# DeltaNet with a hard-swish MLP: block products by eleven from block 3, GpSimd's shared additions in two operations, and another pacing of the inversion

## The chip, the core and the metric

The kernel runs on one core of a Trainium2 chip (trn2). The metric is device time in microseconds of one execution. The profile names the engines PE (TensorE), PEld (its weight loads), DVE (VectorE), ACT (ScalarE), POOL (GpSimd) and SP (SyncE, which issues the transfers).

## The reference

Two stages in float32. The first is a delta-rule attention over 4 x 8 heads, 768 tokens, head width 48; the second multiplies its output, as 3072 rows of 384, by two weight matrices with a gate between them:

```python
k_n = k / (norm(k) + 1e-6)
for t in range(768):                     # state: 48 x 48 for each of 32 heads
    y[t]  = q[t] @ state
    state += beta[t] * outer(k_n[t], v[t] - k_n[t] @ state)
x = y.transpose(0, 2, 1, 3).reshape(3072, 384)
h = x @ w_in                             # 384 x 2048
g = h * clip(h + 3, 0, 6) / 6
out = g @ w_out                          # 2048 x 384
```

## The kernel before

**Chunks.** Time is cut into N = 24 chunks of 32 tokens; a chunk holds 4 x 32 = 128 rows on the partitions. For chunk t, `prep` normalises the keys (`kb`, on GpSimd), transposes keys and queries (`pt`), copies them (`KQ`, ScalarE), multiplies them with each other (`sc`) and writes the masked triangles `L` and `LB` on VectorE. The mask times beta (`mb`, function `mask`) and the scaled keys (`bkb`, function `scaled`) are GpSimd's. `chain` then runs the recurrence: `ks` (state times keys and queries) on TensorE, `R` (three VectorE operations at L892 and L898), `pz` (inverse times R, TensorE), `su` (state update, TensorE), `state` (VectorE, L945), and beside them the output: `y` (L811, L854), `py`, and the transposition `yt` into `xT`, the MLP's input.

**Groups.** The triangular inverse X that `pz` needs is made for four chunks at once: groups are chunk 0, chunks 1 to 4, 5 to 8, 9 to 12 and so on. From group 2 on `inverse` does it on VectorE: a transposition in (L461), then 60 column operations in turn (a product L751, a subtraction L756; 30 to 240 elements wide, the widest in the middle), a memset and a transposition out (L465). `pz` of a group's first chunk can't start before that.

**Blocks.** The MLP takes two chunks as a block (256 rows), twelve blocks. The upward product of a block is either `up` (L983: 16 tiles of 3 products 128 columns by 256 rows) or, from block UF = 5 on, `up_by_eleven` (L1055: for each of 8 pairs of tiles, eleven products of 128 x 128 in place of twelve such areas, with sums of the weights, made once by `weight_sums` on GpSimd, and sums of the input, `token_sums` on VectorE). For each pair j, `begin(j)` does four products, which ScalarE copies out (L1069) and GpSimd adds up to shared parts (L1020, in `plus_minus`); `end(j)` does seven more, and VectorE closes with two additions from PSUM (L1085, L1086). ScalarE and VectorE then gate (L1096, L1099; after `up` it is L991 and L994). The downward product from block 2 on is `down_by_seven` (L1211: seven products of half blocks, with sums of g on VectorE, L1197, and additions to the outputs, L1221, most of them by the engine called `near`, GpSimd except in the last block). Two transfers of the outputs, four issues each, follow them.

**Order.** Every engine executes its instructions in the order in which the program writes them. Up to chunk 4 an explicit list sets it. From chunk LS = 5 on a loop over chunks t and NU = 15 units u writes it: each unit takes a step of the chain or of `prep` (`plan`), one unit of the MLP (14 for a downward product, 16 for an upward one, together two chunks), and a number of column operations of the inverse that a budget sets: 

```python
room = max(1.65 - USED[mode["of"]] - CHAIN.get(u, 0), 0.15) / mode["mean"]
due += room * left / max((GS - i) * NU - u, 1)
due = min(due, 3.0)
take(fill, int(due))
```

So an odd chunk goes with a downward product (of block (t - 3)/2), the even chunk after it with the upward product of the next block: chunk 7 with the downward product of block 2, chunk 8 with the upward product of block 3, chunk 11 and 12 with 4 and 5, 15 and 16 with 6 and 7, 19 and 20 with 8 and 9. A group's inverse is spread over the last three chunks of the group before (the one for chunks 9 to 12 over chunks 7 and 8).

## Time and profile before

| what | value |
|---|---|
| median of 3 runs | 677.34 us (676.79 to 678.49) |
| the profiled execution | 677.9 us, its span 676.2 us |
| PE busy | 638.2 us, 94% |
| DVE busy | 500.0 us, 74% |
| ACT, POOL busy | 272.3 us, 221.1 us |
| granted TensorE clock, mean | 0.987 |

The profiled execution lies 0.56 us above the median; 1.7 us of it are outside the span. PE's busy time counts modelled ends, so it is read together with the waits. Busy shares are averages: the first 130 us (loading, converting weights) differ from the stretch from 213 us on, in which a pair of one downward and one upward product repeats about every 50 us.

### The profile page before, as it was taken

How to read it: one execution, taken by the hardware profiler on the slowest of the kernel's cores; microseconds unless marked ns; L12 is line 12 of the kernel's file. 1: busy time of each engine (PE TensorE's matmuls, PEld its weight loads, DVE VectorE, ACT ScalarE, POOL GpSimd, SP SyncE). 2: the span in 40 equal slices, each digit the busy share in tenths (PEclk: the TensorE clock that was granted, in tenths of full speed). 3: DMA queues.
4: the chain of work that ended last, by engine and by line, in shares of the span. 5: the costliest groups of instructions: out<-in, count | busy, mean ns of one | idle time of the engine just before them, and what ended most of it. 6: DMA issues, size and time to landing. Idle time of an engine off the chain costs nothing.

```text
span 676.2 us, 26940 instructions
## 1 busy us (share of the span) xinstructions
PE 638.2 (94%) x11768; PEld 579.8 (86%) x11768; DVE 500.0 (74%) x1226; ACT 272.3 (40%) x532; POOL 221.1 (33%) x376
## 2 busy tenths in 40 slices
PE   2568989999999999999999999999999999999997
PEld 2457977776689988988999999999999999999997
DVE  5998867888546699747888957998747998557264
ACT  5995767422143132232244244244244143143250
POOL 6230232002521121236165255065052151442340
PEclk9978989999999999999999999999999999999999
DMA  7896435402041030032030030020020020010000
GB/s 190 214 231 147 97 75 147 82 1 48 17 87 22 3 71 3 2 72 37 3 71 4 3 73 2 3 61 2 3 49 3 2 49 2 15 25 3 26 1 23
DMA packets 88501, 33.29 MB, mean 49 GB/s; under 512 B 80160, under 2 KB 83232, under 8 KB 88384
## 3 DMA queue, kind: packets, MB, share of 16 engines
q1 hardware_dynamic: 88128, 31.29, 20.4%
q8 instruction: 92, 1.51, 0.9%
q10 hardware_dynamic: 256, 0.30, 0.2%
q14 instruction: 25, 0.20, 0.1%
HBM read 26.84 MB, written 4.72 MB: 47 GB/s over the span
## 4 chain that ended last, share of the span: by engine, by line
PE 82%; DMA 6%; DVE 6%; issue 2%; ACT 1%; SPq 1%; POOL 1%; DVEq 0%; ACTq 0%; POOLq 0%
PE po L1211 27%; PE ph L1055 17%; PE ph L983 15%; PE po L1146 6%; PE ks L798 3%; DMA w_out<-in_moe_w_in_dram 3%; PE py L819 3%; PE pz L819 3%; PE su L927 3%; PE pt L518 2%; PE sc L539 2%; DMA qb<-in_q_dram 1%; PE yt L864 1%; DVE A L756 1%; DVE pr L751 1%
## 5 line engine op out<-in xcount | busy, mean ns | idle before, releaser
L1055 PE MATMUL ph<-xT,w_in 128*128 128x128 f32 x784 | 122.9, 278 | 0.0
L983 PE MATMUL ph<-xT,w_in 128*128 128x256 f32 (+1 forms) x576 | 117.0, 356 | 0.7 <-ACT spare L348 0.5
L1211 PE MATMUL po<-w_out,g 128*128 128x192 f32 x640 | 110.6, 326 | 0.0
L983 PEld LDWEIGHTS ph<-xT,w_in 128*128 128x128 f32 x576 | 96.3, 197 | 12.6 <-DVE g L994 0.6
L1055 PEld LDWEIGHTS ph<-xT,w_in 128*128 128x128 f32 x784 | 103.9, 192 | 1.3
L1020 POOL TENSOR_TENSOR g<-g 128x128 f32<-128x128 f32 x168 | 79.7, 476 | 75.4 <-ACT g L1069 66.2
L1211 PEld LDWEIGHTS po<-w_out,g 128*128 128x128 f32 x640 | 104.1, 190 | 0.2
L1211 PE MATMUL po<-spare,g 128*128 128x192 f32 x480 | 86.7, 332 | 0.0
L1211 PEld LDWEIGHTS po<-spare,g 128*128 128x128 f32 x480 | 77.2, 190 | 1.8
L1221 POOL TENSOR_TENSOR o<-o,u 128x192 f32<-128x192 f32 x18 | 18.6, 1035 | 167.2 <-ACT o L1218 93.5
L991 ACT ACTIVATE g<-ph,halves 128x256 f32<-128x256 f32 (+1 forms) x96 | 41.2, 437 | 78.3 <-PE ph L983 78.1
L1069 ACT ACTIVATE g<-ph 128x512 f32<-128x512 f32 x56 | 33.4, 597 | 80.5 <-PE ph L1055 77.0
L1197 DVE TENSOR_TENSOR g<-g 128x256 f32<-128x256 f32 x160 | 62.7, 440 | 3.5 <-PE po L1211 3.1
L756 DVE TENSOR_TENSOR A<-A,pr 128x30 f32<-128x30 f32 (+9 forms) x150 | 59.5, 397 | 3.6
L751 DVE TENSOR_TENSOR pr<-A 128x30 f32<-128x30 f32 (+9 forms) x150 | 56.1, 374 | 3.4
L994 DVE SCALAR_TENSOR_TENSOR g<-g,ph 128x256 f32<-128x256 f32 (+1 forms) x96 | 35.0, 371 | 25.2 <-ACT g L991 24.7
L348 ACT ACTIVATE spare<-spare,places 128x768 uint16<-128x768 uint16 (+1 forms) x56 | 52.5, 941 | 1.6 <-DMA spare<-in_moe_w_in_dram 0.6
L1099 DVE SCALAR_TENSOR_TENSOR g<-o,g 128x512 f32<-128x512 f32 x56 | 42.5, 759 | 6.6 <-ACT o L1096 6.6
L1218 ACT ACTIVATE o<-po 128x192 f32<-128x192 f32 x40 | 13.3, 331 | 80.5 <-PE po L1211 76.3
L1146 PE MATMUL po<-w_out,g 128*128 128x384 f32 x128 | 45.6, 493 | 0.0
L1096 ACT ACTIVATE o<-g,halves 128x512 f32<-128x512 f32 x56 | 40.5, 722 | 12.6 <-DVE g L1099 8.9
L478 POOL TENSOR_TENSOR mb<-beta_tok,mask 128x256 f32<-128x256 f32 x38 | 27.0, 730 | 55.8 <-DVE LB L550 55.8
(141 smaller groups left out, 985.2 us busy)
## 6 DMA issues: line engine op xcount, KB each, us to landing
kf<-in_k_dram SPq DMA_DIRECT2D x96, 48.0 KB, 2.8
qb<-in_q_dram SPq DMA_DIRECT2D x96, 48.0 KB, 2.8
vf<-in_v_dram SPq DMA_DIRECT2D x96, 48.0 KB, 2.1
out_dram<-o SPq DMA_DIRECT2D x92, 48.0 KB, 1.6
spare<-in_moe_w_in_dram SPq DMA_DIRECT2D x4, 768.0 KB, 7.7
w_out<-in_moe_w_in_dram SPq DMA_DIRECT2D x4, 768.0 KB, 8.0
w_out<-in_moe_w_out_dram SPq DMA_DIRECT2D x4, 768.0 KB, 5.6
spare<-in_moe_w_out_dram SPq DMA_DIRECT2D x4, 768.0 KB, 4.4
```

Of the source, the lines that this page charges most:

```text
L348: nc.scalar.activation(out=z, in_=z if n else d.bitcast(I16)[:, :, :, 3], func=func, bias=places[:, n : n + 1], scale=scale,)
L751: nc.vector.tensor_tensor(out=pv, in0=A[:, j + 1 :, j].unsqueeze(2).to_broadcast([n, w, j]), in1=A[:, j, 0:j].unsqueeze(1).to_broadcast([n ...
L756: nc.vector.tensor_tensor(out=A[:, j + 1 :, 0:j], in0=A[:, j + 1 :, 0:j], in1=pv, op=ALU.subtract)
L819: nc.tensor.matmul(ps[rows(place(b)), D * h : D * h + D], lhsT=m(h)[rows(b)], rhs=z[rows(b), D * at(h) : D * at(h) + D], start=True, stop= ...
L983: nc.tensor.matmul(ph[:, cols], lhsT=w_in[:, s, f * 128 : (f + 1) * 128], rhs=xT[:, s, cols], start=(s == 0), stop=(s == NKT - 1),)
L991: nc.scalar.activation(out=g, in_=ph, func=ACTF.Relu, bias=half, scale=1.0 / 6.0)
L1020: nc.gpsimd.tensor_tensor(out=out, in0=a, in1=b, op=op)
L1055: nc.tensor.matmul(ph[:, n], lhsT=w, rhs=x, start=start, stop=stop, skip_group_check=True)
L1099: nc.vector.scalar_tensor_tensor(out=g, in0=r, scalar=1.0, in1=g, op0=ALU.min, op1=ALU.mult)
L1146: nc.tensor.matmul(pos[c][:], lhsT=gs[blk, f // 2][:, f % 2, c * P : (c + 1) * P], rhs=w_out[:, f, :], start=(f == 0), stop=(f == NFC - 1),)
L1197: nc.vector.tensor_tensor(out=A(f, *out), in0=A(f, *a), in1=A(f, *b), op=op)
L1211: nc.tensor.matmul(ps[n][:], lhsT=A(f - f % 2, *a)[:, f % 2], rhs=b[:, f], start=(f == 0), stop=(f == HF - 1),)
```

## The change

Five edits. (1) `up_by_eleven` from block 3 on in place of 5, which moves `weight_sums` from the downward product of block 4 to that of block 2 and brings `token_sums` to blocks 3 and 4. (2) The shared parts of a pair in two GpSimd operations (one of 128 x 256, one of 128 x 128) in place of three of 128 x 128, and the closing additions in the other order. (3) All `near` additions on VectorE. (4) The GpSimd masks two units later, after the copy of the transposed keys. (5) Another budget for the columns: other means, more units marked in CHAIN, and half a unit less in units 11 to 13 of odd chunks.

```diff
-        if whole:
-            drain(mask(t))
         yield                                   # prep, after kb
...
+            if whole and j == 0:
+                drain(mask(t))                  # prep, after the copy of KQ
             yield
...
-    mode = {"of": "down", "mean": 0.72}
+    mode = {"of": "down", "mean": 0.6}
...
-    UF = 5
+    UF = 3
...
-            plus_minus(gt[:, 1], gt[:, 1], gt[:, 2], ALU.add)
-            plus_minus(gt[:, 2], gt[:, 0], gt[:, 1], ALU.add)
-            plus_minus(gt[:, 0], gt[:, 0], gt[:, 3], ALU.add)
+            plus_minus(gt[:, 3:1:-1], gt[:, 0:2], gt[:, 3:1:-1], ALU.add)
+            plus_minus(gt[:, 0], gt[:, 0], gt[:, 2], ALU.add)
...
-            nc.vector.tensor_tensor(out=gt[:, 3], in0=ph[:, 3], in1=gt[:, 2], op=ALU.add)
             nc.vector.tensor_tensor(
                 out=gt[:, 1:3], in0=ph[:, 1:3],
-                in1=gt[:, 0].unsqueeze(1).to_broadcast([128, 2, P]), op=ALU.add,
+                in1=gt[:, 3].unsqueeze(1).to_broadcast([128, 2, P]), op=ALU.add,
             )
+            nc.vector.tensor_tensor(out=gt[:, 3], in0=ph[:, 3], in1=gt[:, 0], op=ALU.add)
...
-        near = nc.gpsimd if blk + 1 < N // CB else nc.vector
+        near = nc.vector
...
-            mode["mean"] = 0.72 if blk + 1 < UF else 0.45
+            mode["mean"] = 0.6 if blk + 1 < UF else 0.4
...
-        CHAIN = {1: 0.75, 2: 0.75, 3: 0.4, 4: 0.4, 6: 0.8, 9: 0.8, 10: 0.8}
+        CHAIN = {
+            0: 0.8, 1: 0.8, 2: 0.7, 3: 0.4, 4: 0.4, 5: 0.4, 6: 0.4, 9: 0.8, 10: 0.8, 13: 0.3, 14: 0.4
+        }
...
-                room = max(1.65 - USED[mode["of"]] - CHAIN.get(u, 0), 0.15) / mode["mean"]
+                room = max(1.65 - USED[mode["of"]] - CHAIN.get(u, 0) - (0.5 if t % CB and 10 < u < 14 else 0), 0.15) / mode["mean"]
```

Counted in the programs, between the R of one chunk and the R of the next, the column operations fall so: 

| | chunk 7 | 8 | 9 | 10 | 11 | 12 | 14 | 15 | 16 | 18 | 19 | 20 |
|---|---|---|---|---|---|---|---|---|---|---|---|---|
| before | 27 | 31 | 0 | 16 | 26 | 18 | 15 | 26 | 19 | 15 | 26 | 19 |
| after | 24 | 32 | 4 | 11 | 22 | 27 | 11 | 22 | 27 | 11 | 22 | 27 |

(two of the first group lie in chunk 6 before the change).

## The prediction

> **What bounds the kernel.** I read the page first (busy shares, slices), then busy time by stretches, one from each block's first downward product to the next. DVE 74% as a mean hides that it is nearly full wherever an inverse runs:

> ```profile
> PE 638.2 (94%) x11768; PEld 579.8 (86%) x11768; DVE 500.0 (74%) x1226; ACT 272.3 (40%) x532; POOL 221.1 (33%) x376
> ...
> 213.07:264.88 51.81, 51.58 (x872) 46.11 (x871) 42.10 (x110) 14.39 (x31) 9.75 (x14) 1.00 0.12 25
> 264.88:316.02 51.14, 51.14 (x872) 46.27 (x871) 33.16 (x76) 14.57 (x32) 22.04 (x31) 1.00 0.19 37
> 316.02:367.25 51.23, 50.53 (x952) 48.51 (x951) 44.61 (x112) 17.73 (x37) 21.13 (x37) 1.00 0.12 26
> 367.25:417.48 50.23, 50.19 (x953) 48.38 (x951) 37.20 (x85) 19.27 (x40) 23.15 (x41) 1.00 0.13 26
> 417.48:469.63 52.15, 50.51 (x951) 48.46 (x951) 47.79 (x119) 19.07 (x39) 22.33 (x39) 1.00 0.10 21
> ```

> After the interval the columns are PE, PEld, DVE, ACT, POOL busy, clock, DMA. PE is the bound, with no gap in the second row and few elsewhere; the clock is full. An undisturbed stretch with `up` takes 51.14 us, one with eleven 50.23. DVE has 4 to 7 us left where an inverse runs (rows 3 and 5).

> Next the chain that ended last, for what each product costs TensorE when nothing interrupts it:

> ```profile
> 297.82 2.59 PE ph L983 x12
> ...
> 634.50 19.71 PE ph L1055 x176
> ```

> Then the timelines of DVE and PE over chunks 11 to 13:

> ```profile
> 347.96 0.52 DVE L756 TENSOR_TENSOR A<-A,pr 128x210 f32<-128x210 f32 x1
> 348.40 0.73 DVE L892 SCALAR_TENSOR_TENSOR R<-ks,parity,vf 128x192 f32<-128x192 f32 x2
> 351.71 0.74 DVE L811 SCALAR_TENSOR_TENSOR y<-ks,parity,y 128x192 f32<-128x192 f32 x2 [0.79 <-ACT y L835]
> 365.80 0.29 DVE L1085 TENSOR_TENSOR g<-ph,g 128x128 f32<-128x128 f32 x1 [1.13 <-PE ph L1055]
> 366.46 1.23 DVE L1099 SCALAR_TENSOR_TENSOR g<-o,g 128x512 f32<-128x512 f32 x1
> 373.40 1.99 DVE L465 STREAM_TRANSPOSE X<-A 128x1024 f32<-128x1024 f32 x1
> 376.49 0.62 DVE L898 SCALAR_TENSOR_TENSOR R<-ks,parity,R 128x384 f32<-128x384 f32 x1
> ...
> 453.64 0.88 PE L819 MATMUL pz<-R,X 32*32 32x48 f32 x64 [0.83 <-DVE R L898]
> ```

> Two deadlines tie DVE to PE. `pz` of an even chunk waits for R, which stands behind columns (first line): PE stood 0.15, 0.83 and 0.83 us for it, in chunks 12, 16 and 20. `pz` of a group's first chunk waits for the transposed inverse and R behind it: R ended at 377.1, `pz` started at 377.25, so nothing is in hand there.

> **TensorE's work.** `up` is 96 passes at 2.59/12 = 0.216 us: 20.7 us. Eleven is 176 passes in 19.71. A block gains 1.0 us (the two undisturbed stretches differ by 0.91; I use 0.95), two blocks 1.9. In the last stretch weight loads were busy 19.52 of 19.71 us, so narrower products save less than their columns: by columns alone 176 x 0.108 = 19.0 would save 1.7 a block. [...] The trace's spacing is 112 ns, and the sum uses it.

> **VectorE's work.** An eleven block costs 8 x (0.285 + 0.425 + about 0.74) = 11.6 us and 1.9 of token sums, against 16 x 0.417 = 6.7 for `up`: +7 us in each of blocks 3 and 4. The five `near` additions cost DVE 0.355 each (the last block's), 1.8 a block, and GpSimd loses 4.0 (1.04 + 0.64 and so on). These lie in odd chunks, where DVE waits 1 to 3 us a chunk for products; price if that is gone: 1.8 a block. The outputs' transfers wait for the last but one of them. On SP eight issues (4.3 us) and then the loads of v and q stand behind; R of the even chunk doesn't use those loads (at 396.11 it ran while they were being issued), so a few tenths of delay are covered by a chunk.

> **GpSimd.** A pair goes from three operations (1.52 us) to 0.73 (the 128x256 row of the weight sums) + 0.45: 0.3 less, 2.7 an even chunk. Its effect is through DVE: operations with both inputs in SBUF run slower while GpSimd works (L756 0.53 against 0.35, L1099 1.23 against 0.68), those from PSUM don't. The weight sums (16 x 0.73 = 11.7 us) move to chunk 7, where POOL is busy 9.8 of 51.8; kb, mask and bkb queue behind some, and are early by more than 5 us. Masks later: shared parts stop queueing behind 1.2 us of mask; L waits for `sc` anyway. All at nothing; were the cover gone, 1 to 2 us once for the sums.

> **Columns.** This decides. Ahead of R in chunk 12 twelve columns stood after the last output addition; five will, so R comes right after `ks`, and the 1.81 us of PE waits go. But DVE then idles: R is done at about D + 29.7 (D is the block's first downward product), and the next closing pair needs `end(1)`, at D + 32.1 (399.38 - 367.25 in chunk 14, which has no columns there). `y` starts when ScalarE has its part, at D + 35.7 (351.71 - 316.02) in either kernel. Behind `y` in chunk 12 stand 26 columns instead of 18: 8 x 0.43 = 3.4 us more. Waits in that stretch absorb 0.45 + 1.13 = 1.6. So X, and `pz` of chunk 13, come 1.8 us later than D + 61.2.
> Chunk 17: R of chunk 16 had been late, `y` at D + 36.8 comes 1.1 earlier, waits absorb 0.45 + 0.80: 3.4 - 1.3 - 1.1 = +1.0. Chunk 21: waits 0.19 + 1.15, `y` 0.8 earlier: +1.3.
> Chunk 9, whose group runs through blocks 2 and 3 in two chunks only: behind `y` of chunk 8 stand 29 columns and 4 more after it, 15 more than in chunk 12's pattern, 15 x 0.43 = 6.5. D + 61.2 + 6.5 - 1.6 = D + 66.1, against D + 61.7 before (274.77 - 213.07): +4.4. Block 4's gain of 0.95 follows in the next stretch; block 3's is inside.
> Sum: 4.4 + 1.8 + 1.0 + 1.3 - 0.95 = +7.5.

> Against it: GpSimd slowed DVE in chunk 12 by about 2.5 us (three gatings 0.5 each, columns 1.0). How much of that remains no row shows. Bounds: all (0 gained) or none (2.5 a group, 10 in all). In proportion to GpSimd's time (15.0 to 12.3 us an even chunk) 0.45 would go; with the mask no longer ahead of the shared parts, and the gatings elsewhere in the queue, I take 1.0 a group, 4.0 in all. That gives +3.5: 677.9 + 3.5 = 681.4 for a profiled execution, 0.56 less for the median, **680.8**.

> **Rivals.** (a) *VectorE catches up*: with contention gone as good as wholly (over 2 us a group, the point from which it decides) X is in time in chunks 13, 17 and 21 and TensorE's own work sets the pace: -1.9 for two blocks, -1.81 for R, -0.44 for the wait in chunk 15 at 427.88, all of it lost again only where chunk 9 waits. Full: 677.3 - 4.2 = 673.2; with 1.9 lost in chunk 9: 675. For it: the second row above, with GpSimd busy 22.04 us but mostly outside DVE's busy spells, has no PE gap at all. Against: the anchors at D + 32.1 and D + 35.7 are TensorE's and ScalarE's, whatever DVE has left, and the columns stand behind them.
> (b) *Work saved and columns late cancel*: contention falls by about 1.7 a group, +0.7: 678.
> (c) *Odd chunks lose as well*: 3 more columns and one output addition stand ahead of `y` in chunks 11, 15 and 19 (16 against 13): 1.65 us later, where chunk 15 had no idle time in its queue; `yt` and `begin(0)` then wait, up to 1.3 a group: 680.8 + 4 = 684.8.

> **How the numbers follow.** Forecast 0.45, (a) 0.30, (b) 0.20, (c) 0.05. The range 673.0 to 684.0 takes in (a) and contention unchanged (684.8) but for its end. A measurement of this kernel tells about 0.3% (2 us) from no change: faster 0.30 is (a), same 0.21 is (b) and the edge of the forecast, slower 0.49 is the rest.

> **What would show it.** Right: PE waits of 3 to 5 us at `pz` of chunk 9 (releaser R or the transposition) and 1 to 2 us in chunks 13, 17 and 21; none at `pz` of 12, 16, 20; DVE idle 2 us after R there; DVE over 48 us in the stretches of chunks 7 to 8. Wrong: PE without gaps there, stretches of 50.2 us from block 2 on, or L756 and L1099 at their undisturbed 0.35 and 0.68 throughout.

## The result, and the profile after

The changed kernel took **696.76 us** (median of 4 runs, 695.79 to 698.13) against 677.37 before (4 runs): ratio **1.0286**, 95% interval 1.0263 to 1.0309. Slower was the right side, but the prediction had 680.8 and a range that ended at 684.0. The loss is 19 us, not 3.5.

First the page of the kernel after, its busy shares and one of its DMA queues (packets, MB, share):

```profile
PE 641.1 (92%) x11928; PEld 587.5 (85%) x11928; DVE 516.8 (74%) x1295; ACT 280.7 (40%) x548; POOL 193.7 (28%) x307
...
q8 instruction: 94, 1.54, 0.9%
```

PE is busy only 2.9 us longer than before, in a span that is 17.9 us longer: TensorE mostly waits. The second line becomes important below. Busy time by stretches, cut at the first downward product of each block (columns as in the prediction: PE, PEld, DVE, ACT, POOL, clock, DMA):

```profile
214.07:270.30 56.23, 52.16 (x952) 50.07 (x950) 45.40 (x112) 17.71 (x37) 23.05 (x35) 0.97 0.12 24
270.30:326.27 55.97, 52.69 (x953) 50.76 (x951) 41.98 (x101) 19.28 (x40) 17.51 (x27) 0.94 0.17 34
326.27:379.96 53.69, 50.97 (x952) 48.44 (x951) 46.18 (x119) 18.74 (x39) 15.61 (x25) 1.00 0.12 25
379.96:431.64 51.68, 50.19 (x953) 48.38 (x951) 38.56 (x95) 19.16 (x40) 18.64 (x28) 1.00 0.12 25
```

Before, these four took 51.81, 51.14, 51.23 and 50.23 us. The clock, 1.00 in all four before, is 0.97 and 0.94 in the first two. Where TensorE stands still, the timeline of PE shows (in brackets: idle time ahead, and what ended it):

```profile
252.37 0.34 PE L539 MATMUL sc<-KQ 64*32 64x64 f32 x14 [1.88 <-issue]
264.29 0.52 PE L864 MATMUL yt<-ident,y 128*128 128x128 f32 x3 [2.19 <-DVE y L854]
283.70 1.50 PE L819 MATMUL pz<-R,X 32*32 32x48 f32 x64 [3.28 <-DVE X L465]
364.32 0.33 PE L539 MATMUL sc<-KQ 64*32 64x64 f32 x10 [0.97 <-issue]
375.56 0.55 PE L864 MATMUL yt<-ident,y 128*128 128x128 f32 x3 [1.52 <-DVE y L854]
391.58 0.88 PE L819 MATMUL pz<-R,X 32*32 32x48 f32 x64 [1.49 <-DVE R L898]
```

Three kinds of stop: `pz`, which the prediction named; `yt`, which it did not; and stops inside `sc`, between two of 64 like products, with no releaser ("issue"). The first two come again in chunks 16 and 17 (1.55, 1.49) and 20 and 21 (1.69, 0.80). The third line has one thing more: the same 64 products take 1.50 us there and 0.88 in the last. The clock says why:

```profile
264.00:265.50 1.50, 1.21 (x11) 1.24 (x12) 1.47 (x5) 0.49 (x1) 0.00 (x0) 1.00 0.00 0
265.50:267.00 1.50, 1.50 (x9) 1.50 (x9) 1.47 (x4) 1.20 (x3) 0.56 (x1) 0.52 0.00 0
267.00:268.50 1.50, 1.50 (x9) 1.50 (x8) 0.44 (x1) 0.28 (x1) 1.42 (x3) 0.50 0.00 0
...
286.00:287.50 1.50, 1.50 (x27) 1.33 (x12) 1.20 (x5) 0.00 (x0) 0.00 (x0) 0.50 0.00 0
```

Behind the 2.19 us at `yt` the granted clock is 0.50 until about 269, behind the 3.28 at `pz` until about 289: 1.7 and 2.9 us lost, worked out from busy time and clock of 1.5 us slices.

The balance from 214 to 672 us: stops at `yt` 6.95, at `pz` 7.06, inside `sc` 2.85, one of 0.23 for `KQ`, together 17.1 against 3.4 before; plus 4.6 for the clock; less 1.8 that eleven saves in the two blocks (x1 below). That makes 16.5; the stretches grew by 16.7. (Another 1.2 us lies ahead of 214 us, where traces differ by up to 6.)

### The profile page after: what moved, and what is told of

Its sections match the earlier page's. It is cut to its first block, busy times and chain, and to the rows that moved or that the text cites. A ratio compares the mean times of both kernels' runs of the same rounds, so it can differ in the third digit from the quotient of the medians.

```text
span 694.1 us, 27284 instructions
## 1 busy us (share of the span) xinstructions
PE 641.1 (92%) x11928; PEld 587.5 (85%) x11928; DVE 516.8 (74%) x1295; ACT 280.7 (40%) x548; POOL 193.7 (28%) x307
## 3 DMA queue, kind: packets, MB, share of 16 engines
q8 instruction: 94, 1.54, 0.9%
## 4 chain that ended last, share of the span: by engine, by line
PE 75%; DVE 15%; issue 4%; ACT 3%; DMA 1%; SPq 0%; POOL 0%; DVEq 0%; ACTq 0%; POOLq 0%
PE po L1210 23%; PE ph L1055 21%; PE ph L983 8%; PE po L1145 6%; PE pz L819 3%; PE ks L798 3%; DVE A L756 2%; PE sc L539 2%; PE py L819 2%; PE pt L516 2%; DVE g L1098 2%; DVE pr L751 2%; PE su L927 2%; ACT spare L348 1%; DVE g L1084 1%
## 5 line engine op out<-in xcount | busy, mean ns | idle before, releaser
L1020 POOL TENSOR_TENSOR g<-g 128x256 f32<-128x256 f32 (+1 forms) x144 | 87.4, 608 | 292.4 <-ACT g L1069 286.8
L1055 PE MATMUL ph<-xT,w_in 128*128 128x128 f32 x1008 | 159.8, 280 | 0.4 <-ACT KQ L524 0.2
L1055 PEld LDWEIGHTS ph<-xT,w_in 128*128 128x128 f32 x1008 | 135.0, 193 | 2.4 <-ACT KQ L524 0.8
L1069 ACT ACTIVATE g<-ph 128x512 f32<-128x512 f32 x72 | 43.0, 597 | 109.5 <-PE ph L1055 106.4
L1084 DVE TENSOR_TENSOR g<-ph,g 128x256 f32<-128x256 f32 x72 | 30.2, 420 | 61.7 <-PE ph L1055 40.3
L983 PE MATMUL ph<-xT,w_in 128*128 128x128 f32 (+1 forms) x384 | 71.2, 337 | 2.3 <-DVE g L994 1.6
L983 PEld LDWEIGHTS ph<-xT,w_in 128*128 128x128 f32 x384 | 59.4, 195 | 9.5 <-DVE g L994 2.0
L756 DVE TENSOR_TENSOR A<-A,pr 128x30 f32<-128x30 f32 (+9 forms) x150 | 59.6, 398 | 3.6
L1098 DVE SCALAR_TENSOR_TENSOR g<-o,g 128x512 f32<-128x512 f32 x72 | 53.1, 738 | 7.7 <-ACT o L1095 7.6
L1095 ACT ACTIVATE o<-g,halves 128x512 f32<-128x512 f32 x72 | 52.0, 723 | 11.8 <-DVE g L1098 7.4
L1055 PE MATMUL ph<-beta_tok,sums_in 128*128 128x128 f32 x288 | 55.7, 275 | 0.0
L1055 PEld LDWEIGHTS ph<-beta_tok,sums_in 128*128 128x128 f32 x288 | 43.7, 192 | 0.0
L524 ACT ACTIVATE KQ<-pt 128x512 f32<-128x512 f32 x48 | 27.8, 593 | 36.3 <-PE pt L516 35.7
```

The lines of the kernel that those rows point to most:

```text
L756: nc.vector.tensor_tensor(out=A[:, j + 1 :, 0:j], in0=A[:, j + 1 :, 0:j], in1=pv, op=ALU.subtract)
L983: nc.tensor.matmul(ph[:, cols], lhsT=w_in[:, s, f * 128 : (f + 1) * 128], rhs=xT[:, s, cols], start=(s == 0), stop=(s == NKT - 1),)
L1020: nc.gpsimd.tensor_tensor(out=out, in0=a, in1=b, op=op)
L1055: nc.tensor.matmul(ph[:, n], lhsT=w, rhs=x, start=start, stop=stop, skip_group_check=True)
L1069: nc.scalar.activation(out=gt, in_=ph[:], func=ACTF.Copy)
L1095: nc.scalar.activation(out=r, in_=g, func=ACTF.Relu, bias=half, scale=1.0 / 6.0)
```

## The experiments

The medians of before were 679.9 to 680.5 us on the chips that ran these, so ratios are compared; an expectation in us stands for its ratio to 677.4. Durations of stretches come from one trace for each kernel. Where no stop lies in them they agree from kernel to kernel (51.14, 51.14 and 51.13 for chunks 9 and 10 in the table), but stops inside `sc` differ between kernels with the same products (0.97 to 2.07 us in chunk 12), and the traced execution of e2 lay 4.2 us above its median. The eight from chunk 7 to chunk 22, summed: before 399.6, the changed kernel 416.3.

| stretch (chunks) | before | f1 budget | e1 all but UF | e4 UF alone | after | x1 after, no columns |
|---|---|---|---|---|---|---|
| 7, 8 | 51.81 | 51.63 | 52.14 | 56.58 | 56.23 | 51.93 |
| 9, 10 | 51.14 | 51.14 | 51.13 | 53.25 | 55.97 | 50.11 |
| 11, 12 | 51.23 | 52.15 | 51.84 | 55.21 | 53.69 | 51.64 |
| 13 to 22 | 245.4 | 250.2 | 249.9 | 245.4 | 250.4 | 244.0 |
| sum | 399.6 | 405.2 | 405.0 | 410.4 | 416.3 | 397.7 |

### The change taken apart: e1, e4, f1, e2, e3, g1

**e1_uf5**, the changed kernel with `up` back in blocks 3 and 4:

```diff
-    UF = 3
+    UF = 5
```

> The changed kernel with eleven products from block 5 again (UF = 5), all else as changed. Theory 1 (columns behind y: the budget puts 8 more columns behind y of chunks 12, 16 and 20, and the eleven products of block 3 on top of that overload chunk 8): the two stretches from block 2 on, 9.2 us over before in the changed kernel, come back, the three groups after that stay: 696.8 - 9.2 = 687.5, with waits of TensorE at yt of chunks 12, 16, 20 (1.5 us each) and at pz of chunks 13, 17, 21. Rival A (the near additions on VectorE are what delays y): 690 or more, since blocks 2 and 3 keep them too. Rival B (the eleven products in blocks 3 and 4 alone): back to 677 to 679.

Measured 1.0079 (1.0041 to 1.0117), less than theory 1 had (687.5, ratio 1.015) and more than rival B. The stops are those of theory 1: the first two stretches come back, and `yt` and `pz` of the later groups still wait (1.50, 1.56, 1.70 and 1.15, 1.49, 0.78). **e4_uf3_only**, the kernel before with edit (1) alone:

```diff
-    UF = 5
+    UF = 3
```

> The kernel before with eleven products from block 3 on, all else as before. Theory 1: chunk 8 has 27 columns and the closings behind y, chunk 9 is late by about half of what the changed kernel shows, the groups after that are as before: 677.4 + 3 to 5 = 680 to 682, with a TensorE wait at pz of chunk 9 of 1 to 3 us. Rival B (block 3 alone costs the whole of the 9.2 us): 686. Rival C (TensorE's saved work is worth its 1.9 us because the old budget keeps VectorE in time): 675.5.

Measured 1.0178 (1.0132 to 1.0224), above all three expectations. Two stops inside `sc` (2.04 and 1.97 us in chunks 8 and 12), each with half clock behind it, were in none of them; `pz` of chunk 9 waits 2.12. **f1_pace_only**, the kernel before with edit (5) alone:

```diff
-    ... CHAIN = {1: 0.75, 2: 0.75, 3: 0.4, 4: 0.4, 6: 0.8, 9: 0.8, 10: 0.8}; means 0.72, 0.45
+    ... CHAIN as in the change; means 0.6, 0.4; 0.5 less in units 11 to 13 of odd chunks
```

> The kernel before with the new budget for columns alone (the dictionary, the 0.5 for odd chunks, 0.6 and 0.4). Theory (the budget costs what is left of the loss when blocks three and four keep up): as e1, ratio 1.007, waits at yt of chunks 12, 16 and 20 (1.5 us) and at pz of 13, 17 and 21 (0.8 to 1.5 us). Rival (two-operation shared parts, masks or the near additions cost it): ratio 1.000 to 1.003, no wait over 0.8 us at yt.

Measured 1.0098 (1.0062 to 1.0133), with the stops it was to have (the `yt` of chunks 16 and 20 1.56 and 1.03, `pz` of 17 and 21 1.76 and 0.78):

```profile
366.17 0.55 PE L864 MATMUL yt<-ident,y 128*128 128x128 f32 x3 [1.50 <-DVE y L854]
382.12 0.88 PE L819 MATMUL pz<-R,X 32*32 32x48 f32 x64 [1.43 <-DVE R L898]
```

So the loss has two parts that add up. The budget costs 5.6 us of stretches (f1 less before); eleven from block 3 costs 11.3 (after less e1) or 10.8 (e4 less before); the other three edits together nothing beside the new budget (e1 less f1: -0.1). Beside the old one the traces have 1.5 us (g1 less before) and 3.1 (e2 less e4) for them; the medians of e2 and e4, 1.0140 and 1.0178, don't bear out the second.

**e2_pace_b**, the changed kernel with the budget of before (f1's diff, reversed):

> The changed kernel with the budget of before (means, CHAIN, no subtraction in odd chunks), all else as changed. Columns then: 30 and 27 in chunks 7 and 8, 26 and 19 in chunks 11 and 12. Theory 1 (budget): the waits at yt of 12, 16, 20 and pz of 13, 17, 21 go (3.0 us a group, 7.5 in all with what the later stretches show), and of the 9.2 in blocks 2 and 3 half goes with 5 columns fewer behind y and no clock loss: 684 to 685; R of even chunks waits behind columns again (0.8 each). Rival A (near additions): 693 or more. Rival B (eleven products in blocks 3 and 4): 687, the first two stretches unchanged at 56 us.

Measured 1.0140 (1.0087 to 1.0192). The stops at `yt` of 12, 16 and 20 and `pz` of 13, 17 and 21 go, but for 0.2 us, and those at `pz` of 12, 16 and 20 return (1.10, 1.23, 1.63), with one at `pz` of 8 (1.74). The first two stretches give back half of the 9.2 us, as theory 1 had it (55.49 and 52.04). By time it is rival B all the same (1.0140 is 687): stops inside `sc` of chunks 12 and 16 (2.07, 1.85), each with half clock behind it, come on top. **e3_near_b**, the changed kernel with `near` on GpSimd again:

```diff
-        near = nc.vector
+        near = nc.gpsimd if blk + 1 < N // CB else nc.vector
```

> The changed kernel with the near additions on GpSimd again, all else as changed. Theory 1 (columns behind y): near additions lie in odd chunks, in which VectorE waits for products, so little changes: 694 to 697. Rival A (near additions delay VectorE into the even chunk, 1.8 us a block): 696.8 - 4 x 1.8 = 689 to 690 or lower.

Measured 1.0264 (1.0218 to 1.0310), not to be told from the changed kernel: the additions cost nothing. **g1_two_mask**, edits (2) and (4) on the kernel before (their lines as in the change):

> The kernel before with the shared parts in two GpSimd operations (and the closing additions that go with them) and the masks later; budget, near additions and the number of up blocks stay. Theory: these two cost nothing, 0.998 to 1.001, since GpSimd is not on the path and the budget alone (1.0098) was as dear as everything but the up blocks (1.0079). Rival (they shift work into VectorE's busy spells, as e2 against e4 could be read): 1.003 to 1.005, with longer waits in front of pz of chunks 12, 16 and 20 than 0.8 us.

Measured 1.0029 (1.0007 to 1.0051), just under the rival's range: a little slower, where the theory expected nothing. `pz` of chunks 12 and 20 waits 1.10 and 1.23, as the rival had it; in chunk 16 it is `KQ` that waits, 1.31.

### With VectorE out of the way: x1, x2

**x1_nocol_after** and **x2_nocol_before** skip the columns of the four inverses from chunk 9 on:

```diff
         for j in range(1, C - 1):
             w = C - 1 - j
+            if first(g) >= 9:
+                yield
+                yield
+                continue
```

> The changed kernel without the column operations of the inverse for the groups that begin with chunk 9 and later (their two VectorE operations a column are left out, the schedule's places for them stay). Theory one (VectorE's queue: the columns stand ahead of what TensorE waits for): the waits of TensorE in front of yt and pz from 260 us on go, and with them the half clock behind the two longest: 2.2 + 3.3 + 1.5 + 1.5 + 1.6 + 1.5 + 1.7 + 0.8 = 14.1 us, and about 3 us for the clock, so about 679.5, ratio 1.003; the two stops inside sc (1.9 and 1.0 us, released by nothing in the profile) stay at the same matmuls. Rival (TensorE's own side or the data's arrival is what makes it late): over 690, ratio over 1.018, waits in front of yt and pz still there.

> The kernel before without the same column operations. Only its own waits can go (0.2 + 0.15 + 0.8 + 0.4 + 0.8 = 2.4 us): 675, ratio 0.9965. Beside x1 it gives what eleven products in blocks three and four are worth with VectorE out of the way: the prediction said 1.9 us less; with the stops in sc that the changed kernel shows (2.9 us in all) x1 would come out 1 us above x2, without any other loss.

x1: 0.9984 (0.9955 to 1.0014). x2: 0.9934 (0.9904 to 0.9964). Both are a little under what was expected (1.003 and 0.9965). All waits for VectorE go, and no slice of 5 us between 200 and 670 shows a lower clock. The stretch of chunks 9 and 10, of x1 and then of x2:

```profile
266.54:316.65 50.11, 50.11 (x952) 48.35 (x951) 36.98 (x83) 19.25 (x40) 19.36 (x29) 1.00 0.19 38
```

```profile
266.94:318.07 51.13, 51.13 (x871) 46.27 (x870) 30.44 (x65) 14.57 (x32) 22.02 (x31) 1.00 0.19 37
```

Both full. Eleven saves 1.02 us in block 4, as predicted (0.95), and 0.8 in block 3 (51.93 less its stop of 1.59, against 51.13 in x2). x1 has only the stops inside `sc` left, 1.59, 1.29 and 1.50 us in chunks 8, 12 and 16, more than the two blocks save. The eight stretches are 2.9 us longer in x1 than in x2 (397.7 against 394.8), and 16.7 with the columns. So most of the change's loss needs the columns in VectorE's queue; the stops inside `sc` do not.

### The stops inside sc: p1

How many TensorE records lie ahead of such a stop, read as the first count in the row from 0 to just before it: after (chunk 8), e4 (chunk 8), x1 (chunk 16).

```profile
0.00:252.30 252.30, 218.59 (x4796) 180.03 (x4797) 190.12 (x470) 128.15 (x229) 76.44 (x126) 0.99 0.41 95
```

```profile
0.00:256.10 256.10, 221.99 (x4796) 183.25 (x4797) 196.03 (x473) 128.64 (x229) 81.25 (x135) 0.95 0.41 94
```

```profile
0.00:456.30 456.30, 421.18 (x8604) 374.94 (x8605) 311.39 (x746) 204.65 (x387) 145.79 (x230) 0.99 0.29 65
```

Where eleven starts with block 3, such stops come at 4796 in chunk 8, 6700 in chunk 12 and 8604 in chunk 16, and in the first 100 us of all kernels at some of 349, 475, 727, 853, 979 and 2002 (the changed kernel has all six): mostly steps of 126 to 127 or a multiple, and 11928 records over the 94 packets of queue q8 are 126.9. So the stops are as far apart as one packet of that queue (1.54 MB / 94 = 16 KB) is long, counted in records. **p1_pad18** moves the program against that grid:

```diff
-            for p in range(NP):
+            for p in [0] * (18 if t == j == 0 else 0) + list(range(NP)):
                 nc.tensor.transpose(
```

> The changed kernel with the first of the transpositions into pt in chunk 0 issued 18 times more at the start (the same result written again), so that everything behind it on TensorE stands 18 matmuls later in the instruction stream; the trace shows each as two records, 36 in all. Theory (the stops without a releaser sit at fixed places of the instruction stream: in every kernel so far behind records 349, 475, 727, 853, 979, 2002, 4796, 6700, 8604, many of them multiples of 126 to 127 apart): the stops in sc of chunks 8 and 12 go, others may turn up 36 records earlier in the sequence. If they lie on the path that sets the end, 1 to 3 us less than the changed kernel, ratio to before 1.024 to 1.027; where the wait in front of yt of chunk 8 only grows by what the stop loses, the first 1.9 us bring nothing. Rival (the stop belongs to sc, to its banks or its operands): they stay in sc of chunks 8 and 12.

Measured 1.0303 (1.0264 to 1.0342). The padding made 18 records (11946 in place of 11928), not 36. `sc` of chunks 8 and 12 runs whole, and a stop shows in chunk 13, which had none; behind it the count:

```profile
253.56 0.86 PE L539 MATMUL sc<-KQ 64*32 64x64 f32 x64
...
393.97 0.21 PE L539 MATMUL sc<-KQ 64*32 64x64 f32 x1 [2.10 <-issue]
```

```profile
0.00:393.90 393.90, 352.65 (x7208) 309.11 (x7209) 304.92 (x750) 177.57 (x332) 122.02 (x192) 0.94 0.31 70
```

7208 is 6700 + 4 x 127: the new stop lies on the same grid, so the stops belong to places in the instruction stream and not to one `sc`. The longest of them after 200 us took 2.66 us (k1, below).

Why a place stops TensorE in one kernel and not in another, the times of the packets of q8 in the traces say. From 200 us on the kernels have 33 stops of this kind of 0.25 us or more. Each ended 1.2 to 1.6 us after the transfer of a packet had ended, and 2.3 to 2.9 us after it had begun. In the changed kernel that packet came from 249.81 to 250.92 us, and TensorE, which had reached 4796 at 250.49, went on at 252.37. In d1 (below) the packet was there at 251.04 and TensorE reached the same product at about 252.9; in p1, where 4796 still lies inside `sc` of chunk 8 (records 4764 to 4828), the packet was there at 250.03 and TensorE at about 254.0. Neither stopped. So in these three traces TensorE stood where it came to the place before the packet had landed, and ran on where it came after. `pz` and `sc` use up 128 records in 1.6 us (as do `su` and `py`), less than the 2.3 to 2.9 us from a packet's start to the end of a stop; 128 products of L1055 take an estimated 14 us (at 19.71/176 each). What sets the moment at which a packet is called for the runs do not say.

The padding brought no time: the waits at `yt` and `pz` of chunks 8 and 9 grew to 2.58 and 3.68, and three new stops came.

### What a stop costs beside its length: t1

**t1_stops** is x2 with the first two operations of R repeated in six even chunks:

```diff
+            for e in [0, 1] * {10: 4, 12: 5, 14: 6, 16: 7, 18: 8, 20: 10}.get(t, 0):
+                nc.vector.scalar_tensor_tensor(...)   # as the two of R above
```

> What a stop of TensorE costs beside its length: the kernel of x2 (no columns from the group of chunk 9 on, so no waits of its own), with the first two operations of R issued again 4, 5, 6, 7, 8 and 10 times in chunks 10, 12, 14, 16, 18 and 20, 0.33 us each operation, so that pz comes late by some 1.7, 2.3, 3.0, 3.6, 4.3 and 5.6 us, each stop alone, 50 us from the next. Theory (a stop of about 2 us or more can halve the granted clock for some 3.5 us, and one of over 3 us does): full clock in chunk 10, 0.5 for 3 to 6 us after the last three, the rest open; x2 plus the stops (20.5 us) plus 1.7 to 3 us for each halved clock: 701 to 708. Rival (the drops in the runs so far had another cause, such as two stops close together): clock 1.00 throughout, 695.

Measured 1.0403 (1.0370 to 1.0436), 707.3 us. Chunk 10 had room for its repetitions; the others stopped PE for 2.14, 3.29, 3.55, 5.86 and 6.33 us. Clock behind the first two and in the fourth:

```profile
356.55:358.05 1.50, 1.50 (x128) 1.44 (x128) 1.47 (x5) 0.49 (x1) 0.00 (x0) 1.00 0.51 98
...
410.03:411.53 1.50, 1.50 (x72) 1.38 (x79) 1.47 (x5) 0.00 (x0) 0.00 (x0) 0.50 0.46 87
...
526.13:527.63 1.50, 1.50 (x9) 1.50 (x8) 0.00 (x0) 0.93 (x3) 0.28 (x1) 0.50 0.00 0
```

Against x2 the stretches grew by 2.56, 4.65, 6.49, 8.81 and 8.60 us: the stop of 2.1, with one of 0.24 for `KQ` in the same stretch, costs 0.2 more than the two, one of 3.3 costs 1.4 more, the longer ones 2.3 to 3.0 more.

Length alone does not decide: 2.19 us was enough in the changed kernel at 264, while 2.58 (p1) and 3.29 (e3) passed at full clock. The traces show more. In each of them the granted clock changes only at times that lie a multiple of 3.41 us apart; in the changed kernel that is at 265.56, 268.97, 282.62 and 289.45. Read in these windows, the 2.19 us of the changed kernel fall into one, and the 3.29 us of e3 into two:

```profile
262.14:265.56 3.42, 1.27 (x12) 1.30 (x13) 3.28 (x9) 0.49 (x1) 0.45 (x1) 1.00 0.00 0
265.56:268.97 3.41, 3.41 (x19) 3.41 (x18) 1.99 (x5) 1.49 (x3) 2.45 (x4) 0.50 0.02 5
```

```profile
280.33:283.74 3.41, 1.46 (x9) 1.17 (x8) 3.31 (x11) 0.91 (x2) 1.42 (x2) 1.00 0.00 0
283.74:287.15 3.41, 2.07 (x131) 1.94 (x132) 3.41 (x9) 0.49 (x1) 0.00 (x0) 1.00 0.02 5
```

From 115 to 660 us the 20 traces hold 3037 such windows at full clock. All 16 in which PE stood for 1.96 us or more had half clock in the next, and none with less than 1.62 had. Of the 19 between, 8 had: they held 41 to 130 products, mostly short ones, and 10 of the other 11 held 9 to 16 wide ones. So what told these stops apart was how much of one fell into a single window and, between 1.62 and 1.96 us, which products stood beside it.

### Block four alone, and the weight sums: u4, b1, s1

**u4_uf4_only** is the kernel before with UF = 4; **b1_uf4_two_mask** adds edits (2) and (4).

```diff
-    UF = 5
+    UF = 4
```

(What these expectations call chunks 10 and 11 is the stretch from 264.7 us, chunks 9 and 10 in the table; likewise one chunk less for the one ahead of it.)

> The kernel before with eleven products from block four on (the stretch of chunks 10 and 11, where no inverse is due; block three, in the stretch of chunks 8 and 9 that ends with an inverse, keeps up). Theory (block three is what pushes the inverse; block four alone has room): the stretch of chunks 10 and 11 goes from 51.1 to 50.2 us, ratio 0.997 to 0.9995; a stop at a page of instructions can take 1 to 2 us of it away, since everything behind stands 80 records later. Rival (any eleven block where up stood costs VectorE more than it has): a wait of over 1 us at yt or pz in chunks 10 to 13, ratio over 1.003.

> Both together: eleven from block four on, two-operation shared parts and late masks, on the kernel before. If both theories hold, as u4 within 0.002: 0.996 to 1.000, the candidate for a version that beats both.

u4 1.0063 (1.0043 to 1.0083), b1 1.0108 (1.0081 to 1.0136): both missed. u4 has the rival's ratio without its waits: none over 0.4 us at `yt` or `pz` in chunks 10 to 13, but 1.52 for `KQ` of chunk 12. b1 loses as u4 does, 1.7 us more in front of products of `up`, with half clock behind 1.68 us at `pz` of chunk 20. u4 lost 1.8 us in the stretch of chunks 7 and 8, where it still has `up`. Its timeline there, GpSimd and VectorE:

```profile
260.28 0.75 POOL L1020 TENSOR_TENSOR sums_in<-w_in,sums_in 128x256 f32<-128x256 f32 x1
260.69 0.57 DVE L756 TENSOR_TENSOR A<-A,pr 128x210 f32<-128x210 f32 x1
260.99 0.86 POOL L1020 TENSOR_TENSOR w_in<-w_in 128x256 f32<-128x256 f32 x1
261.30 0.77 DVE L751 TENSOR_TENSOR pr<-A 128x198 f32<-128x198 f32 x1
262.10 0.77 DVE L756 TENSOR_TENSOR A<-A,pr 128x198 f32<-128x198 f32 x1
...
265.17 0.54 DVE L854 TENSOR_TENSOR y<-y,py 128x384 f32<-128x384 f32 x1
```

The weight sums, written down with the next downward product, ran 11 us ahead of it on an idle GpSimd, beside the columns: the product of 198 columns took 0.77 us, and 0.37 in the kernel before. **s1_uf4_sums_late** makes the sums wait for the last `up`, and puts `near` on VectorE:

```diff
-        for j in range(0, NPR, 2):
+        for j in range(NPR - 2, -1, -2):
```

> The kernel before with eleven products from block four on, the near additions on VectorE, and the weight sums taken from the last slices of the weights first, so that they have to wait until the last up block has read them and run behind the inverse for chunk 9, not beside its columns. Theory (in u4 the sums, running 11 us ahead of their place, slowed the columns of that inverse from 0.35 to 0.75 us each, and that was the wait at yt of chunk 8; the wait for KQ came from ScalarE standing behind an output that the near additions on GpSimd had made late): the stretch from 213 us as before (51.8), the next 50.2 to 50.8, the wait for KQ gone, ratio 0.998 to 1.001. Rival (eleven in block four costs on its own): as u4, 1.004 to 1.006.

Measured 1.0018 (0.9998 to 1.0038). The two stretches are 51.14 and 51.04 (0.77 of it a stop without a releaser), so the first step holds by the waits: none at `yt` of chunk 8 is left. s1 moves two things at once, though, and how much of this the sums alone bring was not run. The second step fell: the wait for `KQ` stayed (1.14 us), with `near` on VectorE. ScalarE stood 1.51 us behind a transfer there. None of the versions that leave nothing out beats the kernel before.

### Why block three is so dear: d1, d2, k1, c1, c3

**d1_no_closings34** leaves the closing additions on VectorE out in blocks 3 and 4:

```diff
+            if blk > 4:
                 nc.vector.tensor_tensor(  # gt[:, 1:3], as before
                 nc.vector.tensor_tensor(  # gt[:, 3], as before
```

> The changed kernel without the two closing additions on VectorE in blocks three and four only (8 pairs of 0.29 + 0.42 us a block, 5.7 us a block, left out); GpSimd's shared parts, the token sums, the budget and TensorE's products stay. Theory (block three overruns VectorE's queue in front of y and of the inverse of chunk 9; its closing additions are the larger part of the 7 us that the prediction counted): of the 5.5 us that TensorE waits at yt of chunk 8 and pz of chunk 9 at least 4 go, and the half clock behind them (3 to 4 us) with them; the stops in sc stay; ratio 1.015 to 1.019 in place of 1.029. Rival (GpSimd's contention or the stops at instruction pages make it late): the waits stay over 4 us, ratio over 1.024.

Measured 1.0218 (1.0181 to 1.0255), by time between the two; the waits, 4.4 us together, are the rival's (over 4):

```profile
263.74 0.55 PE L864 MATMUL yt<-ident,y 128*128 128x128 f32 x3 [1.20 <-DVE y L854]
281.47 1.50 PE L819 MATMUL pz<-R,X 32*32 32x48 f32 x64 [3.21 <-DVE X L465]
```

5.7 us less on VectorE brought only 1.0 us at `yt` and 0.1 at `pz`; the first stretch still gained 4.7 us, as the stop in `sc` of chunk 8 and the first half clock went too. **d2_e4_no_closings34** is the same on e4, whose columns stand where they stood before:

> The fourth cell beside e4 (columns placed as before, closing additions in), the changed kernel (columns later, in) and d1 (columns later, out): the kernel before with eleven from block three and without the closing additions of blocks three and four, so VectorE has 5.7 us a block less to do and the columns stand as in e4 (33 ahead of R of chunk 8, 13 between it and y, 14 behind). If load decides under the old placing, the waits at pz of chunks 8 and 9 (1.4 and 2.1 us in e4) go, ratio 1.004 to 1.010, what is left being the stops in sc and a halved clock; if load decides nothing in either placing, they stay, 1.015 to 1.018.

Measured 1.0116 (1.0069 to 1.0164), a little over the first range:

```profile
252.24 0.88 PE L819 MATMUL pz<-R,X 32*32 32x48 f32 x64 [0.88 <-DVE R L898]
255.88 0.46 PE L539 MATMUL sc<-KQ 64*32 64x64 f32 x14 [2.09 <-issue]
281.87 0.88 PE L819 MATMUL pz<-R,X 32*32 32x48 f32 x64 [0.52 <-DVE R L898]
```

Of e4's 3.8 us at `yt` of chunk 8 and `pz` of 8 and 9, 1.4 are left: under the old placing the load does decide. What is left is mostly stops without a releaser, 2.09, 1.78 and 2.27 us in chunks 8, 12 and 16, each with half clock behind it (a mean of 0.66, 0.66 and 0.73 in 5 us). **k1_early** keeps the work and moves the columns forward (39 of the 60 column operations ahead of R of chunk 8, 1 behind the last part of `y`; in the changed kernel 24 and 20):

```diff
-                room = max(1.65 - USED[mode["of"]] - CHAIN.get(u, 0) ...
+                room = max(1.65 - (0.42 if t < 9 else USED[mode["of"]]) - CHAIN.get(u, 0) ...
```

> The changed kernel with the columns of the inverse for chunk 9 put earlier in VectorE's queue (for chunks under 9 the budget counts an eleven unit as an up unit): 19 column operations remain behind R of chunk 8 in place of 33, one behind y of chunk 8 in place of 20; 39 in place of 24 stand ahead of R of chunk 8. Nothing else moves. Theory (the place of the columns in the queue, not VectorE's total work, makes X of chunk 9 late, since d1 took 5.7 us of VectorE's work away and the wait at pz of chunk 9 stayed at 3.2 us): that wait goes (under 0.5 us) with the half clock behind it, 4 to 6 us less, part of it given back as waits at pz or yt of chunks 7 and 8 (1 to 3 us); ratio 1.020 to 1.025. Rival (VectorE has no room wherever they stand): what goes at pz of 9 comes back in full in front of R and y of chunks 7 and 8, ratio 1.027 to 1.031.

Measured 1.0259 (1.0208 to 1.0310), which lies in neither range, so time alone does not tell the two apart. By the stops both are half right: `yt` of 8 and `pz` of 9 wait no longer, and in their place stands

```profile
255.70 0.88 PE L819 MATMUL pz<-R,X 32*32 32x48 f32 x64 [2.06 <-DVE R L898]
259.92 0.46 PE L539 MATMUL sc<-KQ 64*32 64x64 f32 x14 [2.66 <-issue]
```

with half clock until about 265.7. The two stretches fell from 112.2 to 110.0 us, e1 has 103.3. With block 3 by eleven, VectorE can be late at R or at X, and was in both places tried.

**c1_no_shared34** and **c3_no_shared** leave GpSimd's shared parts out, in blocks 3 and 4 and in all:

```diff
+            if blk > 4:   # c3: both lines go
                 plus_minus(gt[:, 3:1:-1], gt[:, 0:2], gt[:, 3:1:-1], ALU.add)
                 plus_minus(gt[:, 0], gt[:, 0], gt[:, 2], ALU.add)
```

> The changed kernel without GpSimd's shared parts in blocks three and four only (8 pairs of operations of 1.3 us, 10.4 us of GpSimd a block, left out); VectorE's closing additions stay. Rival to d1's theory (contention): the 60 column operations of the inverse for chunk 9 take 24.1 us in the changed kernel and 23.2 before, so contention explains 1 us of them, and some of L1098 (0.5 us each slowed pass, 4 or 5 of them): 2 to 3 us less at pz of chunk 9, ratio 1.023 to 1.027. If contention were the cause, the waits at yt of 8 and pz of 9 would go, ratio under 1.019.

> The changed kernel without GpSimd's shared parts in any block. It bounds from the far side what the prediction called relief (none to 2.5 us a group; 1.0 taken): if all of 2.5 us a group were to be had, the waits at yt and pz of chunks 12, 13, 16, 17, 20 and 21 (8.6 us) would go almost wholly, ratio about 1.010 together with blocks three and four; if columns stand late whatever GpSimd does, 1 us a group, ratio about 1.020.

c1 1.0207 (1.0162 to 1.0252), 0.2 points below its expectation; `pz` of chunk 9 waits 2.02, `yt` of 8 1.76, and the 60 columns take 21.6 us in place of 24.1. c3 1.0166 (1.0129 to 1.0204), between its two cases; in the groups of chunks 13, 17 and 21 the waits at `yt` and `pz` sum to 4.4 us against 8.6 in c1.

Of the 5.5 us at `yt` of chunk 8 and `pz` of chunk 9 in the changed kernel, 4.4 stay without the closing additions (d1) and 3.8 without GpSimd's shared parts (c1), and k1 moves them to `pz` of chunk 8. So VectorE's load, the place of the columns and GpSimd beside them all have a part in what block 3 costs; how large each is the runs do not separate.

## Why the prediction was wrong, step by step

- **TensorE's work** (0.95 less a block): right, 1.02 in block 4 and 0.8 in block 3 between x1 and x2.
- **VectorE's +7 us a block**: right in amount (57.6 us busy from 214 to 284 against 49.9 from 213 to 275, up to `pz` of chunk 9 in both). The sign "DVE over 48 us" did not come (45.40 in the stretch of chunks 7 and 8), since part of block 3's closings lies behind that stretch. That it would be late by 4.4 us at `pz` of chunk 9 was also near: 3.28.
- **R in time in chunks 12, 16 and 20**: right, no wait there, and VectorE idle behind R.
- **Columns late at pz of 13, 17 and 21** (1.8, 1.0, 1.3): near, 1.49, 1.49 and 0.80. The step that failed is the one beside it, "Waits in that stretch absorb 0.45 + 1.13". Those were VectorE's waits for TensorE's products. The closing part of `y` (L854) stands behind columns too (in chunk 12 13 of them between R and it, 10 before), so TensorE stood still first, at `yt` (2.19, 1.52, 1.55, 1.69), and its products came later with it. Of these 6.95 us the sum had none. Of the 3.4 us of columns in chunk 12 TensorE lost 1.52 + 1.49 = 3.0, so by these numbers the waits absorbed 0.4 and not 1.6. f1 shows the stops with no block changed: 1.50, 1.56 and 1.03 at `yt`.
- **Relief from GpSimd** (1.0 a group, 4.0 in all): failed. With GpSimd's shared parts gone altogether, three groups gain 4.2 us (c3 against c1), 1.4 a group, where the upper bound was 2.5. The edit takes 18% of GpSimd's time (15.0 to 12.3 us), so about 0.25 a group, an estimate; the prediction had worked out 0.45 in proportion and then took 1.0. Without the relief its sum was +7.5.
- **Not in the sum at all**: the stops without a releaser (2.85 us in the profiled execution, 0.55 before) and the half clock behind windows with a long stop (4.6 us). Both were to be seen before: the kernel's own trace had 0.55 us without a releaser inside `py` at 359.84, and stops of 3.15 and 1.94 us of that kind in its first 100 us. Eleven puts 80 records more into a block, which moves all later products against the steps of 127 records at which the stops come.
- **Weight sums "at nothing"**: the bound "1 to 2 us once" was the right size for it, as u4 shows (1.8); that they run beside columns was missed. In the changed kernel they run at 201 to 222 us; what they cost there was not measured apart.
- **Near additions, masks, two operations**: near additions nothing that shows (e3), the other two together 0.3% (0.1 to 0.5) on the kernel before (g1).
- **Rivals (a) and (b)** needed 2 and 1.7 us of relief a group and fell with it.
- **Rival (c)**, odd chunks lose as well, 4 us, had the right direction and the wrong place: it is the even chunk's `y`.

The account closes: the sum without relief had 8.5 at `pz` less 0.95. Measured were 7.06 at `pz` less 1.8 for both blocks; before's own waits, 2.85 without the stop in `py`, go as well (the sum had set them against the delays of chunks 17 and 21 alone); and 6.95 at `yt`, 2.3 more without a releaser, 4.6 of clock and 0.2 for `KQ` were left out of it. 7.06 - 1.8 - 2.85 + 6.95 + 2.3 + 4.6 + 0.2 = 16.5, against 16.7 in the stretches.

## What to carry to other kernels

An engine's waits are slack only if what they wait for doesn't itself wait for that engine: before counting them as absorbing anything, look for another product of the delayed queue (here `y` for `yt`, 6.95 us of stops) that the other side needs sooner. A stop of TensorE of 2 us or more can have a price beside its length: here the 2.19 us at `yt` brought 1.7 us of loss by half clock and the 3.28 us at `pz` 2.9, while 3.29 us in e3 brought none; with short products beside it, 1.68 us had half clock behind it (b1). And stops without a releaser are worth counting in instructions: where they lie a fixed number apart, as here at 126 to 127 records, an edit that adds products can move them, as the 18 records of p1 did.
